# ScalarE's last copy of a chunk's first unit, placed behind the first copy of the next inner product

## The chip, the cores and the metric

The kernel runs on one core of a Trainium2 chip. The metric is the device time of one execution in microseconds (us), the median of several runs. Lower is better.

## The reference

Two blocks follow one another. The first is a retention layer: for 4 batches and 8 heads, over 768 positions of 64 dimensions, a state per head decays by a factor and takes up the outer product of key and value; the query reads it. The second is a dense pair of layers on the 3072 resulting rows of 512, with a leaky rectifier between.

```python
for t in range(S):
    state = gamma[None, :, None, None] * state + np.einsum('bhd,bhe->bhde', k[:, :, t], v[:, :, t])
    y[:, :, t] = scale * np.einsum('bhd,bhde->bhe', q[:, :, t], state)
...
h = x @ w_in                       # 512 -> 2048
g = np.maximum(0.01 * h, h)
return (g @ w_out).astype(np.float32)   # 2048 -> 512
```

## The kernel before

The sequence is cut into 6 chunks of 128 positions; with 4 batches a chunk has 512 rows. The hidden layer's 2048 columns are cut into 4 units of 512. For each chunk and unit the kernel makes the hidden values g (first layer and rectifier) and then their part of the output (second layer), which is summed over the units into a tile o of four quarters in SBUF.

All products are made by seven smaller products in place of eight, named M1 to M7, whose sums and differences are made by ScalarE and VectorE or by accumulation in PSUM. From chunk 2 on (the steady part, 4 chunks of 4 units, n = 0 to 15, chunk c = 2 + n // 4, unit u = n % 4) the first layer uses two levels of this:

- `inner_steps(n, group)` makes, one product per step, the seven inner products of one group (4 outer products in group 0, 3 in group 1). It uses PSUM banks 0 to 3. After M1, ScalarE copies bank 0 into bank 3 (line 1185, the "M1 copy"), and M6 is then accumulated into bank 3. After M5, M4, M6 and M2, ScalarE copies a bank into the SBUF tile `made` (lines 1187, 1189, 1191, 1193). M3 accumulates into the bank of M5, M7 into bank 3.
- `outer(n, group)` puts the results together on VectorE; for group 1 ScalarE applies the leaky rectifier to each quarter of g (line 1223, four activations, the "leakies").
- `output(...)` makes the second layer's seven products with `seven` (matmuls at line 662) in banks 4 to 7, in the order M1, M5, M6, M2, M7, M3, M4 (`FUSED`). M4 is the last. Its result is in bank 6, into which ScalarE has first copied M7 (line 773).
- `begin(i, ps)` takes a product into the quarter o[i]. In the first unit of a chunk (`first`, u == 0) ScalarE copies it (line 746, the "o copy"); in the later units VectorE adds it.
- `joint_visit` and `scores_of_pair` make the attention of the next chunk, in units 0 and 1 of chunks 2 to 4 ("visits"), with matmuls at lines 369, 380, 427 and 444. POOL makes a small memset in them that orders two groups of matmuls.

There is no planner. Each engine works off its own queue in the order in which the program issues instructions, and waits in that order. The main loop sets it: for unit n, the differences of g on VectorE, the inner products of group 0 for unit n + 1, a visit where there is one, then the output of unit n with the inner products of group 1 for unit n + 1 in its midst, and the last products of the output at the end of the pass. So the end of one pass and the start of the next read on ScalarE: leakies of unit n + 1, the take of M4 of unit n, the copies of the inner products of group 0 for unit n + 2.

```python
INNER = (("M1", 0, 0, 0), ("M5", 1, 3, 2), ("M4", 2, 2, 4), ("M6", 3, 4, 3), ("M2", 0, 1, 1),
         ("M3", 1, 5, 5), ("M7", 3, 6, 6))        # product, bank, weights, moving part
...
            if m == "M1":
                nc.scalar.copy(out=ps[3], in_=ps[0])
            elif m == "M5":
                nc.scalar.copy(out=sums[:, 3], in_=ps[1])
```

The weights of the inner products are streamed from DRAM into `wa` (group 0) and `wb` (group 1) by SP's queue, issued after the products that used the tile last.

Of the kernel before, what the change touches and what calls it, by code (L numbers as in the profile page):

```python
# [22 lines left out]
def kernel(  # L23
# [182 lines left out]
    def new_o(c, name="o"):  # L206
        return work.tile([128, 4, 2, N], FP32, tag=f"o{int(c > 0)}", name=f"{name}_{c}")
# [120 lines left out]
    room = {}  # L328
# [276 lines left out]
    def plus(out, a, b):  # L605
        nc.vector.tensor_tensor(out=out, in0=a, in1=b, op=ALU.add)  # L606
# [27 lines left out]
    ORDER = (0, 2, 1, 3, 4, 6, 5)  # L634
    FIRST = (0, 4, 2, 1, 3, 6, 5)
    FUSED = (0, 2, 1, 4, 5, 6, 3)
    LAST = (0, 2, 1, 3, 4, 5, 6)
# [3 lines left out]
    def seven(tiles, name, takes, takes_piece=None, order=ORDER, room=None):  # L641

        banks = {}

        def bank_of(bank):
            if bank not in banks:
                banks[bank] = room[bank] if room is not None else ffs.tile(
                    [128, 2, N], FP32, tag="ff", bufs=4, name=f"{bank}_{name}")
            return banks[bank]

        which = [("M1", "A", 0, 0), ("M6", "B", 5, 5), ("M5", "C", 4, 4), ("M4", "D", 3, 6),
                 ("M2", "A", 2, 2), ("M7", "B", 1, 1), ("M3", "C", 6, 3)]
        for m, bank, sa, sb in (which[i] for i in order):
            first = bank not in banks
            split = takes_piece is not None and bank == "C"
            ps = bank_of(bank)
            places = zip(ps, PIECES) if split else ((ps[:, i, :], (i, 0, N)) for i in range(2))
            for to, (i, a, z) in places:
                for n, (w, x, t) in enumerate(tiles):
                    rhs = x[:, sb] if sb < 4 else t[:, sb - 4]  # L660
                    for k in range(2):
                        nc.tensor.matmul(  # L662
                            to, lhsT=block(w, sa)[:, k, ts(i, 128)], rhs=rhs[:, k, a:z],
                            start=(first and (i == 0 or split) and n == 0 and k == 0),
                            stop=(n == len(tiles) - 1 and k == 1), skip_group_check=True)
                if split and m == "M3":
                    takes_piece(to, i, a, z)
            if not (split and m == "M3"):
                takes(m, ps, bank_of)
            yield  # L670
# [61 lines left out]

        return seven([(2 * u, x, t)], f"h{at}", takes, order=order)

    def output(c, o, parts, first, final, room=None, order=ORDER):

        at = f"{c}_{parts[0][0]}"
        fused = order == FUSED

        def store(i):  # L740
            if final:
                nc.sync.dma_start(out=out[c, i], in_=o[:, i])

        def begin(i, ps):
            if first:
                nc.scalar.copy(out=o[:, i], in_=ps)
            else:
                add(i, ps)

        def add(i, ps):  # L750
            plus(o[:, i], o[:, i], ps)

        def takes(m, ps, bank_of):
            if m == "M1":
                nc.scalar.copy(out=bank_of("B"), in_=ps)  # L755
            elif m == "M6":
                begin(1, ps)
            elif m == "M5":
                if isinstance(ps, list):
                    for part, (i, a, z) in zip(ps, PIECES):  # L760
                        plus(o[:, 3, i, a:z], o[:, 3, i, a:z], part)
                else:
                    begin(3, ps)
            elif m == "M4":
                begin(2, ps)
                if fused:
                    store(2)
            elif m == "M2":
                begin(0, ps)
                store(0)  # L770
            elif m == "M7":
                if fused:
                    nc.scalar.copy(out=bank_of("D"), in_=ps)  # L773
                add(3, ps)
                store(3)
                if not fused:
                    add(2, ps)
                    store(2)
            elif m == "M3":
                add(1, ps)  # L780
                store(1)

        def takes_piece(ps, i, a, z):
            plus(o[:, 1, i, a:z], o[:, 1, i, a:z], ps)
            queue = nc.scalar if 0 < a else nc.sync
            queue.dma_start(out=out[c, 1][:, i, a:z], in_=o[:, 1, i, a:z])

        return seven([(2 * u + 1, g, gd) for u, g, gd in parts], f"o{at}", takes,
                     takes_piece if final and c == NC - 1 else None, order, room)

# [9 lines left out]
    def new_g(c, u):  # L800
        i = slot[0]
        slot[0] = 1 - i
        g = work.tile([128, 4, 2, N], FP32, tag=f"g{i}", name=f"g_{c}_{u}")
        gd = work.tile([128, 3, 2, N], FP32, tag=f"gd{i}", name=f"gd_{c}_{u}")
        return u, g, gd
# [61 lines left out]
    parts = [new_g(0, 0)]  # L867
# [180 lines left out]
    def at_of(n):  # L1048
        return 2 + n // NU, n % NU
# [76 lines left out]
    for u in range(NU):  # L1126
        for c in range(2) if u > 0 else ():
            if c == 0:
                parts = []
# [38 lines left out]
    def inner(n, group, held=False):  # L1168

        products(inner_steps(n, group, held), 8)  # L1170

    def inner_steps(n, group, held=False):

        c, u = at_of(n)
        w, count = streamed[group], 4 - group
        moving = operands(c, group)
        sums = made_of[group]
        ps = [part[:, 0 : count * C].rearrange("p (i n) -> p i n", n=C) for part in bank[0:4]]
        for m, q, j, s in INNER:
            for i in range(count):  # L1180
                nc.tensor.matmul(ps[q][:, i], lhsT=w[:, j, i], rhs=part_of(moving[i], s),  # L1181
                                 start=(i == 0 and m in ("M1", "M5", "M4")), stop=True,
                                 skip_group_check=True)
# [4 lines that stand above are left out]
            elif m == "M4":  # L1188
                nc.scalar.copy(out=sums[:, 2], in_=ps[2])
            elif m == "M6":  # L1190
                nc.scalar.copy(out=sums[:, 1], in_=ps[3])
            elif m == "M2":
                nc.scalar.copy(out=sums[:, 0], in_=ps[0])
            elif m == "M3":
                plus(sums[:, 1], sums[:, 1], ps[1])
            elif m == "M7":
                plus(sums[:, 3], sums[:, 3], ps[3])
                plus(sums[:, 2], sums[:, 2], ps[3])
            yield
        if not held:  # L1200
            load_unit(n + 1, group)
# [37 lines left out]
    def products(steps, n):  # L1239

        for _ in range(n):
            next(steps, None)
# [7 lines left out]
    room = dict(zip("ABCD", map(halves, (5, 4, 7, 6))))  # L1250
# [20 lines left out]
    begun = inner_steps(1, 0, held=True)  # L1271
    for steps, leakies in ((1, later[:2]), (2, later[2:])):
        products(begun, steps)
        for do in leakies:
            do()

    for n in range(N2):
        c, u = at_of(n)
        more = n + 1 < N2
        if u == 0:  # L1280
            os[c] = new_o(c)
        visiting = c + 1 < NC and u < 2
        if n + 1 < N2:
            differences(*gs[n][1:])
        if n + 1 < N2 and u == NU - 1:
            sums_of_x(c + 1, 1)
        if n + 1 < N2:
            if n == 0:
                products(begun, 5)
            else:  # L1290
                inner(n + 1, 0, held=visiting)
            outer(n + 1, 0)
        if visiting and u == 0:
            xs[c + 1] = new_x(c + 1)
        if visiting:
            joint_visit(c + 1, 2 * u)
        steps = output(c, os[c], [gs.pop(n)], u == 0, u == NU - 1, room=room if more else last_room,
                       order=FUSED if more else LAST)
        products(steps, 3)
        if c + 1 < NC and u < 2 and following(c + 1, 2 * u):  # L1300
            scores_of_pair(*following(c + 1, 2 * u))
        if visiting:
            load_unit(n + 2, 0)
        products(steps, 1)
        if c + 1 < NC and u == 1:
            differences(*xs[c + 1])
        if c + 1 < NC and u == 2:
            sums_of_x(c + 1, 0)
        if more:
            inner(n + 1, 1)  # L1310
            for i in range(2) if visiting else ():
                ahead(c + 2, 2 * u + i)
            products(steps, 1)
            outer(n + 1, 1)
        if n + 2 == N2:
            differences(*gs[n + 1][1:])
        products(steps, 3)
# [92 lines left out]
```

## Time and profile before

| What | Value |
|---|---|
| Runs shown, median (lowest to highest) | 638.59 us (638.56 to 640.17), 4 runs |
| Profiled execution, own time | 638.57 us |
| Span of the profile | 636.8 us |
| Time around the span | 1.77 us |
| TensorE busy, and its weight loads | 630.3 us (99%), 569.2 us (89%) |
| VectorE busy | 462.5 us (73%) |
| ScalarE busy | 269.2 us (42%) |
| Granted TensorE clock, mean | 1.000 |
| M1 copies (line 1185) | 32, of 463 to 592 ns |
| o copies (line 746, by the steady part's names) | 16, of 567 to 588 ns |

The span runs from the first to the last instruction of one profiled execution. Engines are named PE (TensorE's matmuls), PEld (its weight loads, which overlap the matmuls), DVE (VectorE), ACT (ScalarE), POOL (GpSimd) and SP (SyncE). "L1185" is line 1185 of the kernel. A row of a timeline gives the start and the length in us, the engine, the line, the operation, what it writes and reads, how many instructions are merged into the row, and in brackets the idle time before it with what ended it. The ends of matmuls are modelled, so a TensorE that is busy in the page may still have been held up.

### The profile page before, as it was taken

The page shows a single profiled execution, that of the slowest core. Times are in us where ns is not written, and L with a number is a line of the kernel's source. Part 1 is how long each engine was busy: PE and PEld are TensorE (multiplying, and loading weights), DVE is VectorE, ACT ScalarE, POOL GpSimd, SP SyncE. Part 2 cuts the span into 40 slices and gives each one's busy share as a digit, 9 for nine tenths or more (in the row PEclk, how much of TensorE's full clock was granted, in tenths as well). Part 3 has the DMA queues.
Part 4 walks back from the last instruction along what each step waited for, and adds up shares of the span by engine and source line. Part 5 has one row for each costly group of instructions (what it writes and reads, how often), then busy time and mean ns, then how long its engine had stood idle before and what let it go on. Part 6 is the DMA issues. An engine that isn't in the chain of part 4 may idle for free.

```text
span 636.8 us, 14289 instructions
## 1 busy us (share of the span) xinstructions
PE 630.3 (99%) x6086; PEld 569.2 (89%) x6086; DVE 462.5 (73%) x760; ACT 269.2 (42%) x515; POOL 23.4 (4%) x45
## 2 busy tenths in 40 slices
PE   8999999999999999999999999999999999999997
PEld 5888888888888899899999999999999999999996
DVE  5689769889979977476786666877837768636655
ACT  5876556357343124242352352434333423534421
POOL 2000000000011010101000101000010000000000
PEclk9999999999999999999999999999999999999999
DMA  8931327445864998366725382864455336454301
GB/s 332 405 129 43 123 67 235 137 182 183 291 242 127 352 320 275 110 229 200 252 87 194 110 295 84 264 198 135 137 176 176 89 124 194 153 166 154 87 0 67
DMA packets 87536, 113.42 MB, mean 178 GB/s; under 512 B 3240, under 2 KB 71720, under 8 KB 87472
## 3 DMA queue, kind: packets, MB, share of 16 engines
q1 hardware_dynamic: 87168, 111.88, 53.2%
q8 instruction: 48, 0.79, 0.5%
q10 hardware_dynamic: 304, 0.62, 0.3%
q14 instruction: 16, 0.13, 0.1%
HBM read 93.35 MB, written 19.14 MB: 177 GB/s over the span
## 4 chain that ended last, share of the span: by engine, by line
PE 94%; DVE 2%; ACT 1%; DMA 1%; issue 0%; SPq 0%; DVEq 0%; ACTq 0%
PE bank L662 32%; PE bank L1181 27%; PE C_h L662 4%; PE B_o L662 4%; PE A_h L662 4%; PE C_o L662 4%; PE A_o L662 4%; PE B_h L662 4%; PE D_h L662 2%; PE D_o L662 2%; PE d L683 2%; DMA raw<-in_weights_dram 1%; PE bank L369 1%; PE bank L444 1%; PE bank L427 1%; PE bank L380 1%
## 5 line engine op out<-in xcount | busy, mean ns | idle before, releaser
L606 DVE TENSOR_TENSOR made<-made,bank 128x512 f32<-128x512 f32 (+1 forms) x96 | 56.4, 618 | 57.0 <-PE bank L1181 52.6
L606 DVE TENSOR_TENSOR o<-o,bank 128x512 f32<-128x512 f32 (+2 forms) x91 | 58.6, 661 | 53.4 <-PE bank L662 32.8
L662 PE MATMUL bank<-g,w 128*128 128x256 f32 x384 | 89.9, 382 | 0.0
L662 PEld LDWEIGHTS bank<-g,w 128*128 128x128 f32 x384 | 70.7, 190 | 9.2
L1181 PEld LDWEIGHTS bank<-x,wb 128*128 128x128 f32 x672 | 77.6, 192 | 0.8
L1181 PE MATMUL bank<-x,wb 128*128 128x128 f32 x672 | 77.6, 275 | 0.0
L1181 PE MATMUL bank<-x,wa 128*128 128x128 f32 x512 | 68.7, 276 | 0.1
L662 PE MATMUL bank<-gd,w 128*128 128x256 f32 x288 | 66.1, 379 | 0.0
L1181 PEld LDWEIGHTS bank<-x,wa 128*128 128x128 f32 x512 | 63.8, 192 | 1.9 <-ACT bank L1185 0.8
L662 PEld LDWEIGHTS bank<-gd,w 128*128 128x128 f32 x288 | 54.7, 190 | 7.4
L1181 PE MATMUL bank<-t,wa 128*128 128x128 f32 x384 | 53.3, 275 | 0.0
L1223 ACT ACTIVATE g<-g 128x512 f32<-128x512 f32 x64 | 39.3, 631 | 30.8 <-DVE g L606 30.8
L1181 PEld LDWEIGHTS bank<-t,wa 128*128 128x128 f32 x384 | 48.0, 192 | 0.0
L1185 ACT COPY bank<-bank 128x512 f32<-128x512 f32 (+1 forms) x32 | 16.7, 522 | 67.8 <-PE bank L1181 67.5
L606 DVE TENSOR_TENSOR g<-made 128x512 f32<-128x512 f32 x64 | 42.7, 688 | 1.2
L755 ACT COPY bank<-bank 128x512 f32<-128x512 f32 x17 | 9.7, 570 | 71.1 <-PE bank L662 71.0
L609 DVE TENSOR_TENSOR gd<-g,gd 128x512 f32<-128x512 f32 x48 | 33.2, 692 | 5.4 <-ACT g L1223 0.5
L773 ACT COPY bank<-bank 128x512 f32<-128x512 f32 x16 | 9.1, 570 | 46.4 <-PE bank L662 46.4
L662 PE MATMUL bank<-g,last 128*128 128x256 f32 x120 | 28.3, 380 | 0.0
L662 PE MATMUL bank<-gd,last 128*128 128x256 f32 (+1 forms) x124 | 27.5, 373 | 0.0
L662 PE MATMUL A_h<-x,w 128*128 128x256 f32 x112 | 26.6, 380 | 0.0
L662 PEld LDWEIGHTS bank<-gd,last 128*128 128x128 f32 x124 | 22.8, 190 | 3.2 <-DVE gd L609 0.3
(223 smaller groups left out, 1029.1 us busy)
## 6 DMA issues: line engine op xcount, KB each, us to landing
wa<-kept SPq DMA_DIRECT2D x16, 1344.0 KB, 7.2
raw<-in_weights_dram SPq DMA_DIRECT2D x31, 512.0 KB, 4.4
wb<-kept SPq DMA_DIRECT2D x16, 896.0 KB, 5.5
wa<-kept SPq DMA_DIRECT2D x16, 448.0 KB, 4.3
wb<-kept SPq DMA_DIRECT2D x16, 448.0 KB, 6.2
out_dram<-o SPq DMA_DIRECT2D x23, 256.0 KB, 2.5
kept<-w SPq DMA_DIRECT2D x12, 448.0 KB, 5.6
qk<-in_qk_dram SPq DMA_DIRECT2D x10, 512.0 KB, 8.6
```

Of the source, the lines that this page charges most:

```text
L369: nc.tensor.matmul(at[j][ts(h, 64), n, m, i], lhsT=x[ts(j, 64), 1, a, ts(h, 64)], rhs=x[ts(j, 64), 0, a, ts(h, 64)], start=(n == 0 and a = ...
L380: nc.tensor.matmul(sums[h][ts(j, 64), n, a], lhsT=key[ts(h, 64), 2 * a + j], rhs=val[ts(h, 64), 2 * a + j], start=(n == 0 and a == 0), sto ...
L427: mm = nc.tensor.matmul(at[n][j][ts(i, 64), m, ts(h, 64)], lhsT=by_half[h][ts(j, 64), n, a], rhs=x[ts(j, 64), 0, a, ts(h, 64)], start=(n = ...
L606: nc.vector.tensor_tensor(out=out, in0=a, in1=b, op=ALU.add)
L609: nc.vector.tensor_tensor(out=out, in0=a, in1=b, op=ALU.subtract)
L662: nc.tensor.matmul(to, lhsT=block(w, sa)[:, k, ts(i, 128)], rhs=rhs[:, k, a:z], start=(first and (i == 0 or split) and n == 0 and k == 0), ...
L683: nc.tensor.matmul(banks[r][:, i, :], lhsT=block(2 * u, r + 2 * kh)[:, k, ts(i, 128)], rhs=x[:, 2 * kh + th, k, :], start=(step == 0 and i ...
L755: nc.scalar.copy(out=bank_of("B"), in_=ps)
L773: nc.scalar.copy(out=bank_of("D"), in_=ps)
L1181: nc.tensor.matmul(ps[q][:, i], lhsT=w[:, j, i], rhs=part_of(moving[i], s), start=(i == 0 and m in ("M1", "M5", "M4")), stop=True, skip_gr ...
L1185: nc.scalar.copy(out=ps[3], in_=ps[0])
L1223: nc.scalar.activation(g[:, i], g[:, i], AF.Prelu, alpha=0.01)
```

## The change

In units with u == 0 the copy of M4 into o[2] is no longer issued when M4 is made. It is kept in a list. In the next pass the first inner product M1 and its copy are issued first; then the kept copy; then the other inner products with their copies. Only these four copies (n = 0, 4, 8, 12) change their place in ScalarE's queue. In units with u > 0, where VectorE takes M4, the list is empty and the order of instructions stays. For n = 0 the inner products of the next unit were partly issued ahead of the loop already (`begun`), and asking for 7 steps where 5 are left issues the same ones.

```diff
-    def output(c, o, parts, first, final, room=None, order=ORDER):
+    def output(c, o, parts, first, final, room=None, order=ORDER, held=None):
...
             elif m == "M4":
-                begin(2, ps)
+                if held is not None and first:
+                    held.append(lambda: begin(2, ps))
+                else:
+                    begin(2, ps)
                 if fused:
                     store(2)
...
+    held = []
     for n in range(N2):
...
         if n + 1 < N2:
-            if n == 0:
-                products(begun, 5)
-            else:
-                inner(n + 1, 0, held=visiting)
+            if n > 0:
+                begun = inner_steps(n + 1, 0, held=visiting)
+                products(begun, 1)
+            while held:
+                held.pop()()
+            products(begun, 7)
             outer(n + 1, 0)
...
         steps = output(c, os[c], [gs.pop(n)], u == 0, u == NU - 1, room=room if more else last_room,
-                       order=FUSED if more else LAST)
+                       order=FUSED if more else LAST, held=held if more else None)
```

## The prediction

> **What bounds the kernel now.** I read the page first, then the waits of the weight loads, then the order of time on the weight loads and ScalarE around the places that the waits name, and last the same stretch in a unit without that wait.
>
> From the page: the busy row of the engines, the granted clock, and the two rows of the chain that ended last.
>
> ```profile
> PE 630.3 (99%) x6086; PEld 569.2 (89%) x6086; DVE 462.5 (73%) x760; ACT 269.2 (42%) x515; POOL 23.4 (4%) x45
> PEclk9999999999999999999999999999999999999999
> PE 94%; DVE 2%; ACT 1%; DMA 1%; issue 0%; SPq 0%; DVEq 0%; ACTq 0%
> PE bank L662 32%; PE bank L1181 27%; PE C_h L662 4%; PE B_o L662 4%; PE A_h L662 4%; PE C_o L662 4%; PE A_o L662 4%; PE B_h L662 4%; PE D_h L662 2%; PE D_o L662 2%; PE d L683 2%; DMA raw<-in_weights_dram 1%; PE bank L369 1%; PE bank L444 1%; PE bank L427 1%; PE bank L380 1%
> ```
>
> TensorE is the bound, at full clock, and 94% of the chain is TensorE itself. ScalarE is busy 42%, so a copy on it costs nothing by its length. It costs only where TensorE stands still for it. The view of the waits of the weight loads has one row for the copies behind the inner product's M1 (columns: total us, times, longest):
>
> ```profile
> PEld bank L1181 <- ACT bank L1185: 0.8, 4, 0.2
> ```
>
> Four times in 32 copies. The order of time shows all four: 279.78, 381.06, 482.50 and 577.11 us. Each is the inner product that follows the first unit (u = 0) of chunks 2 to 5, and each has the copy of line 746 just ahead of the copy of line 1185. The first of them (columns: start, length, engine, line, what, count, idle before it):
>
> ```profile
> 277.53 1.23 ACT L1223 ACTIVATE g<-g 128x512 f32<-128x512 f32 x2 [0.70 <-DVE g L606]
> 277.71 1.87 PEld L1181 LDWEIGHTS bank<-x,wa 128*128 128x128 f32 x16
> 278.67 0.57 ACT L746 COPY o<-bank 128x512 f32<-128x512 f32 x1
> 279.14 0.59 ACT L1185 COPY bank<-bank 128x512 f32<-128x512 f32 x1
> 279.65 0.59 ACT L1187 COPY made<-bank 128x512 f32<-128x512 f32 x1
> 279.78 1.19 PEld L1181 LDWEIGHTS bank<-x,wa 128*128 128x128 f32 x10 [0.20 <-ACT bank L1185]
> 280.13 0.59 ACT L1189 COPY made<-bank 128x512 f32<-128x512 f32 x1
> 280.89 0.75 PEld L1181 LDWEIGHTS bank<-t,wa 128*128 128x128 f32 x6
> 281.03 0.59 ACT L1191 COPY made<-bank 128x512 f32<-128x512 f32 x1 [0.31 <-PE bank L1181]
> 281.56 0.30 PEld L1181 LDWEIGHTS bank<-x,wa 128*128 128x128 f32 x2
> ```
>
> The 16 loads are M5 and M4; the 10 after the gap are M6 (8) and the start of M2. M6 accumulates into the bank that the M1 copy fills, so it waits until that copy ends at 279.14 + 0.59 = 279.73. The M1 copy stood in ScalarE's queue behind two leaky activations and the o copy; its own input was long there (M5's loads begin at 277.71, after M1's). The same stretch one unit later, where the last second-layer product is added by VectorE and ScalarE has no o copy:
>
> ```profile
> 305.28 1.23 ACT L1223 ACTIVATE g<-g 128x512 f32<-128x512 f32 x2 [0.70 <-DVE g L606]
> 305.46 2.98 PEld L1181 LDWEIGHTS bank<-x,wa 128*128 128x128 f32 x26
> 306.42 0.58 ACT L1185 COPY bank<-bank 128x512 f32<-128x512 f32 x1
> 308.36 0.75 PEld L1181 LDWEIGHTS bank<-t,wa 128*128 128x128 f32 x6
> ```
>
> There the 26 loads run without a gap. Leakies and loads lie to each other as before (305.28 against 305.46; 277.53 against 277.71), so this unit is a model of what the change leaves: the M1 copy follows the leaky at once.
>
> **The change part by part.** Nothing is added or removed. Four ScalarE copies (n = 0, 4, 8, 12) trade places with the M1 copy of the next inner product. No DMA, no VectorE instruction and no matmul moves; SP's and POOL's queues are passed by nothing.
>
> *The M1 copy comes earlier.* From the u > 0 rows it starts 306.42 - 305.28 = 1.14 us after the pair of leakies: 277.53 + 1.14 = 278.67, which is the o copy's present start. It ends by 279.25, and with the 0.05 us from 279.73 to 279.78 M6 is free at 279.30. M6's loads are due at 277.71 + 16 x 0.1115 = 279.49 (0.1115 from 2.90 us for 26 loads). So the wait goes, with 0.19 us to spare.
>
> *What the wait is worth.* Here is the rule that I weigh. The windows from M1's first load to M7's second group of loads, with and without the wait (columns: window, length, busy us of PE, PEld, DVE, ACT, POOL, clock, DMA share, GB/s):
>
> ```profile
> 276.72:282.68 5.96, 5.95 (x52) 5.74 (x51) 4.53 (x8) 4.48 (x9) 0.00 (x0) 1.00 0.73 257
> 304.46:310.15 5.69, 5.69 (x52) 5.66 (x51) 5.14 (x9) 4.11 (x8) 0.00 (x0) 1.00 0.75 252
> ```
>
> By TensorE's busy time the window is full (5.95 of 5.96), and the change would be worth 0.01 us. The Trainium skill, "Perfetto Trace Analysis", section "Identifying the Most-Contended Engine", says that matmul occupancy misleads and that the share of weight loads should be used. By that, idle time falls from 0.22 to 0.03: 0.19 us, four times 0.76. But loads overlap (a load lasts 0.19 and they start 0.1115 apart), so this is short too. The start-to-start length decides: 5.96 - 5.69 = 0.27. From the run of loads after M1 to the second group of M2 it is 280.89 - 277.71 = 3.18 against 2.90: 0.28. The other three give 5.96, 5.96 and 5.96 again. I take 0.275 a piece, 4 x 0.275 = **1.10 us**; ends 0.8 and 1.15.
>
> A second rule would make it more. The skill's "TensorE: Matmul & The Clock Gate", section "A second HAM failure mode: psum-queue depth-cycling", tells of a kernel whose short stops between groups of matmuls let the clock swing between half and full. Part 1 of that page gives a window of about 3.4 us; one such window at half rate after each stop would be worth an estimated 4 x 1.7 = 6.8 us more. In this trace the granted clock is 1.00 in both windows, and the 10 loads after the stop keep the pace. I take nothing for it.
>
> *The o copy comes later.* It moves from 278.67 to about 279.15, behind the M1 copy. A slot is 0.47 us (278.67 to 279.14), not the 0.57 of its row. Its source bank is next written by ScalarE itself, in the copy of line 773 of the next unit (301.42); its target is next touched by VectorE's add in that unit's M4 (306 us). That is over 20 us of cover: nothing. Without cover, 0.5 us each.
>
> *The copies behind it.* Two slots remain two slots, so the M5 copy starts at 279.65 as before, and ends at 280.24. M3 writes its bank, with loads at 281.56 - 0.28 = 281.28: about 1.0 us to spare. The M4 copy also stays; it gives ScalarE free for the M6 copy at about 280.6, and M6 is ready at 281.03 - 0.28 = 280.75. Nothing is pushed.
>
> *A wait passed on.* The o copy now stands behind the M1 copy's wait for M1. M1 is done before the leakies end (278.76), so it waits for nothing; if it did, only this copy and the M5 copy would be behind. All later waits, and the SP issues that TensorE releases, shift with TensorE. After the inner product VectorE waits 1.34 us for M3, then 1.06.
>
> Sum: the profiled execution took 638.57 us (span 636.8, 1.77 around it). 638.57 - 1.10 = 637.47; its time is 0.02 under the median shown, so **637.5** holds for either. That is 0.17%, just under the 0.2% that a measurement of this kernel can tell from no change.
>
> **The rivals.**
>
> *More than the wait* (over 1.28 us). Three visits follow a boundary. In the second, POOL's small memset came 0.94 us after the one before it, against 0.60 and 0.61 in the other two; the 32 loads of line 444 took 0.73 us there against 0.56. Nothing in ScalarE or VectorE explains it. If the shift of 0.28 us undoes it, 0.17 more is won: 637.3. The same chance runs the other way, in two places. A further tenth from the pace after a stop, which the rows model, would also do it. Chance 0.26, at 637.2.
>
> *A part only.* M6 has 0.19 us to spare. If the M1 copy's start slips by 0.3 us, 0.1 us of wait stays at each, 638.0; if the copy is not moved past in effect (a dependence ties both to the same release), 638.6. The u > 0 units, where the copy does start at once in this same company, speak against it. Chance 0.08.
>
> *Slower.* The M5 copy is third behind the leakies, as now, but TensorE arrives 0.28 us earlier at M3, which overwrites its bank. Wait there decides once the M5 copy is over 1.0 us later than now. For a loss of 1.28 us net each boundary needs 0.32 + 0.28 = 0.60 us of wait, so the copy 1.6 us later: 639.9. That is more than three extra slots of ScalarE, and the change adds none. Chance 0.04, and 0.01 for weights that land late: in the second such unit the larger load took 8.6 us from its issue at 395.48, so to 404.1, and is used at 406.23; it is issued behind TensorE's progress and shifts with it.
>
> **How the numbers follow.** The forecast, all four waits gone and nothing in their place: 0.61, at 637.3 to 637.75 (ends 0.8 to 1.25 us). More: 0.26. A part or nothing: 0.08. Slower: 0.05. The range 637.1 to 638.1 leaves out the slower case, half of the partial one and the far end of the first. Faster by over 0.2% is under 637.3: 0.26; slower by over 0.2%: 0.05; between them 0.69.
>
> **What would show it.** In the profile after, the row of weight loads waiting for the copy behind M1 is gone. At the four places the copy of line 1185's counterpart starts about 1.14 us after the pair of leakies, the o copy 0.47 us behind it, and the M5 copy as late as now; 26 loads stand in one run of 2.98 us. The four windows are 5.69 long, and the span is near 635.7. A row of M3 waiting for the M5 copy would prove the slower rival; visit loads of 0.56 or 0.73 us in other places, the first. If the waits are gone and the span is not shorter by 1 us, my step from wait to span is wrong.

## The result and the profile after

| | before | after |
|---|---|---|
| Median | 638.82 us (59 runs) | 637.91 us (39 runs) |
| Lowest | 638.48 us | 637.46 us |
| Ratio of the times, with its 95% interval | | 0.9985 (0.998 to 0.9989) |
| Span of the profiled execution | 636.8 us | 635.9 us |

The change makes the kernel faster by 0.15%, or some 0.96 us; the interval reaches from 0.7 to 1.3 us. The forecast was 1.10 us, 637.5 us, and the measured 637.91 lies in its range. The 59 runs of the kernel before that are counted here have a median 0.23 us above that of the four shown first.

Line numbers past 765 moved: the inner matmuls are now at line 1184, the M1 copy at 1188, the copies of M5, M4, M6 and M2 at 1190 to 1196, the leakies at 1226. The page after, engines and clock:

```profile
PE 629.0 (99%) x6086; PEld 568.8 (89%) x6086; DVE 463.7 (73%) x760; ACT 269.1 (42%) x515; POOL 23.3 (4%) x45
PEclk9999999999999999999999999999999999999999
```

Little is to be seen there: TensorE's busy time is 1.3 us less, at the same clock. What happened is in the view of the waits of the weight loads. All its rows that name a PSUM bank of the steady part (columns: total us, times, longest):

```profile
PEld bank L369 <- issue: 2.0, 6, 0.3
...
PEld bank L662 <- DVE gd L609: 0.3, 1, 0.3
...
PEld bank L427 <- DVE made L606: 0.3, 1, 0.3
...
PEld bank L1184 <- ACT made L1194: 0.2, 1, 0.2
```

The row for the M1 copy, 0.8 us in four waits, is gone, and no row of the steady part is new; the four above were there before. A boundary is, from here on, one of the four places where the inner product behind a chunk's first unit begins. The timeline of the first, weight loads and then ScalarE:

```profile
277.91 2.98 PEld L1184 LDWEIGHTS bank<-x,wa 128*128 128x128 f32 x26
280.81 0.75 PEld L1184 LDWEIGHTS bank<-t,wa 128*128 128x128 f32 x6
281.49 0.30 PEld L1184 LDWEIGHTS bank<-x,wa 128*128 128x128 f32 x2
...
277.73 1.23 ACT L1226 ACTIVATE g<-g 128x512 f32<-128x512 f32 x2 [0.70 <-DVE g L606]
278.87 0.58 ACT L1188 COPY bank<-bank 128x512 f32<-128x512 f32 x1
279.39 0.58 ACT L746 COPY o<-bank 128x512 f32<-128x512 f32 x1
279.87 0.58 ACT L1190 COPY made<-bank 128x512 f32<-128x512 f32 x1
280.34 0.60 ACT L1192 COPY made<-bank 128x512 f32<-128x512 f32 x1
281.24 0.59 ACT L1194 COPY made<-bank 128x512 f32<-128x512 f32 x1 [0.30 <-ACT made L1192]
```

The 26 loads of M5, M4, M6 and the start of M2 stand in one run. The M1 copy follows the pair of leakies by 1.14 us, the o copy it by 0.52, and the M5 copy starts 2.14 us after the leakies (279.87 - 277.73), against 2.12 before. The window of the first boundary, 5.96 us long before, and that of the unit without an o copy, 5.69 long before (columns as before):

```profile
276.92:282.61 5.69, 5.69 (x52) 5.66 (x51) 4.53 (x8) 4.46 (x9) 0.00 (x0) 1.00 0.75 254
304.39:310.08 5.69, 5.69 (x52) 5.67 (x51) 5.13 (x9) 4.11 (x8) 0.00 (x0) 1.00 0.73 246
```

The windows of the other three boundaries, 5.96 us before, are 5.69 each as well. For a sum over all four I take a stretch that leaves out the varying start of the program: from the first loads of line 369 in the first pass of the loop to the loads that wait for VectorE in the last unit. In the kernel before, and then in the one after:

```profile
263.20 1.02 PEld L369 LDWEIGHTS bank<-o 64*64 64x64 f32 x64 [0.33 <-issue]
622.42 5.08 PEld L662 LDWEIGHTS bank<-gd,last 128*128 128x128 f32 x28 [0.34 <-DVE gd L609]
```

```profile
263.40 1.02 PEld L369 LDWEIGHTS bank<-o 64*64 64x64 f32 x64 [0.33 <-issue]
621.54 5.08 PEld L662 LDWEIGHTS bank<-gd,last 128*128 128x128 f32 x28 [0.34 <-DVE gd L609]
```

622.42 - 263.20 = 359.22 us, and 621.54 - 263.40 = 358.14: 1.08 us less, which is four times 0.27. This "loop stretch" is the measure for the experiments too, since the part ahead of it moved from 263.1 to 264.6 us over the profiles of this study, a spread larger than the effect. Three profiles of the changed kernel agree in it to 0.02 us; of the kernel before there is one profile.

### The profile page after: what moved, and what is told of

It is laid out like the page before. It is cut to its first block, busy times and chain, and to the rows that moved or that the text cites. A ratio compares the mean times of both kernels' runs of the same rounds, so it can differ in the third digit from the quotient of the medians.

```text
span 635.9 us, 14285 instructions
## 1 busy us (share of the span) xinstructions
PE 629.0 (99%) x6086; PEld 568.8 (89%) x6086; DVE 463.7 (73%) x760; ACT 269.1 (42%) x515; POOL 23.3 (4%) x45
## 4 chain that ended last, share of the span: by engine, by line
PE 95%; DVE 2%; ACT 1%; DMA 1%; issue 0%; DVEq 0%; ACTq 0%
PE bank L662 32%; PE bank L1184 27%; PE C_h L662 4%; PE B_o L662 4%; PE A_h L662 4%; PE C_o L662 4%; PE A_o L662 4%; PE B_h L662 4%; PE D_h L662 2%; PE D_o L662 2%; PE d L683 2%; PE bank L369 1%; PE bank L444 1%; PE bank L427 1%; PE bank L380 1%; DMA t<-decay_dram 1%
```

## The experiments

The theory: the gain is the wait of M6 for the M1 copy at four places and nothing else, and it passes to the time one for one. The rivals: part of it is given back; the o copy's or the M5 copy's new place matters by itself; the place of the work on ScalarE or VectorE matters.

| Kernel | Loop stretch | Against before | Median | Ratio (95%) |
|---|---|---|---|---|
| before | 359.22 | | 638.82 to 639.09 | 1 |
| after | 358.14 | -1.08 | 637.91 | 0.9985 (0.998 to 0.9989) |
| e1_again | 358.12 | -1.10 | 637.96 | 0.998 (0.9966 to 0.9993) |
| e2_vector | 358.21 | -1.01 | 638.23 | 0.999 (0.9975 to 1.0005) |
| e3_last | 358.21 | -1.01 | 637.77 | 0.9979 (0.997 to 0.9989) |
| e4_twice | 361.69 | +2.47 | 641.50 | 1.0035 (1.0025 to 1.0046) |
| e5_half | 358.66 | -0.56 | 638.50 | 0.9991 (0.998 to 1.0002) |
| e6_two | 358.14 | -1.08 | 637.97 | 0.9981 (0.9972 to 0.999) |
| e7_three | 359.47 | +0.25 | 639.33 | 1.0006 (0.9997 to 1.0014) |
| e8_four | 361.94 | +2.72 | 641.52 | 1.0038 (1.0026 to 1.0051) |
| e9_leaky | 358.13 | -1.09 | 637.22 | 0.9969 (0.9958 to 0.998) |
| e10_again | 358.14 | -1.08 | 638.17 | 0.9985 (0.9973 to 0.9997) |

Times in us. The edits of e2 and e4 are to the kernel before, those of the others to the changed kernel; e1 and e10 are the changed kernel itself. The place that e9 changes lies ahead of the loop stretch. The intervals of e2, e5 and e7 hold 1; for these the loop stretch decides.

**e1_again: the changed kernel, beside e2 to e4.** 

> The changed kernel once more, beside the others. Theory (the whole gain is M6's wait for the M1 copy, 0.27 us at each of four places): 1.1 us under before, a ratio of 0.9983. Rival (part of the gain is lost or given back elsewhere): 0.5 to 0.8 us under before.

The stretch is 1.10 us shorter, the median 1.06 (639.02 to 637.96). The rival of a part given back is not seen in the stretch.

**e2_vector: VectorE takes the copy at its old place.**

```diff
             elif m == "M4":
-                begin(2, ps)
+                if first and fused and c >= JOINED:
+                    nc.vector.tensor_copy(out=o[:, 2], in_=ps)
+                else:
+                    begin(2, ps)
```

> In the kernel before, VectorE instead of ScalarE copies M4 into o[2] in the first unit of chunks 2 to 5, at the old place; ScalarE's queue is free of it. Theory: the same 1.1 us under before, since only the M1 copy's start counts; M6's wait is gone and VectorE's differences of g move 0.6 us later into its 1.34 us of idle time. Rival (the gain needs the copy to stay on ScalarE, because VectorE then becomes late for the visit): under half of the gain, with a new wait of line 427 or 662 for VectorE.

The stretch is 1.01 us shorter and no wait takes the place of the one removed, though the run's ratio alone would not tell it from no change. Its timeline, ScalarE and then VectorE:

```profile
278.05 1.23 ACT L1226 ACTIVATE g<-g 128x512 f32<-128x512 f32 x2 [0.70 <-DVE g L606]
279.19 0.58 ACT L1188 COPY bank<-bank 128x512 f32<-128x512 f32 x1
...
279.13 0.68 DVE L766 COPY o<-bank 128x512 f32<-128x512 f32 x1
...
283.16 2.11 DVE L606 TENSOR_TENSOR made<-made,bank 128x512 f32<-128x512 f32 x3 [0.56 <-PE bank L1184]
```

The M1 copy comes 1.14 us after the leakies, as in the change. VectorE's idle time ahead of M3's add is 0.56 us, where it was 1.34 before and 1.06 in the change: the copy is paid from there. So the gain does not hang on ScalarE keeping the copy, nor on where the copy goes.

**e3_last: the kept copy behind all the inner copies.**

```diff
-            while held:
-                held.pop()()
             products(begun, 7)
+            while held:
+                held.pop()()
```

> The kept copy goes behind all five copies of the inner product instead of behind the first only. Theory: the same as the change, 1.1 us under before, as nobody waits for the o copy. Rival (the copies behind the kept one matter, so M5's copy coming 0.47 us earlier wins something more): 1.3 us under before or better.

1.01 us in the stretch, so the M5 copy's start 0.48 us earlier wins nothing. The 0.07 us by which e2 and e3 fall short of the change arise ahead of the moved copy: in both, M1's first two groups of loads start 0.42 us apart in place of 0.32 at the first boundary, and the windows of the other three are 5.68 to 5.69 us as in the change. What makes that one slip was not tried.

**e4_twice: the copy twice at its old place.**

```diff
                 begin(2, ps)
+                if first and fused and c >= JOINED:
+                    begin(2, ps)
```

> In the kernel before, the o copy is made twice at its old place, so that the M1 copy comes one slot of 0.47 us later still. Theory: M6's wait grows from 0.27 to 0.74 us at each of four places, 4 x 0.47 = 1.9 us over before, a ratio of 1.0030. Rival (the wait is partly hidden or made good later by TensorE): under 1.0 us over before.

It came out 2.47 us over before in the stretch and 2.48 in the medians, more than the 1.9 expected. The timeline says why:

```profile
280.09 1.19 ACT L746 COPY o<-bank 128x512 f32<-128x512 f32 x2
281.17 0.59 ACT L1187 COPY bank<-bank 128x512 f32<-128x512 f32 x1
...
281.82 1.19 PEld L1183 LDWEIGHTS bank<-x,wa 128*128 128x128 f32 x10 [0.81 <-ACT bank L1187]
```

The M1 copy starts 1.08 us after the first o copy, against 0.47 with one: a repeat of the same copy takes 0.61 us and not a slot of 0.47. With 0.61 the wait row says the same: 0.81 - 0.20 = 0.61. Four times 0.61 is 2.44 us. So the wait passes to the time one for one, as the theory has it, and the size that I gave the second copy was wrong.

**e5_half: kept back at two of the four places.**

```diff
-                       order=FUSED if more else LAST, held=held if more else None)
+                       order=FUSED if more else LAST, held=held if n in (0, 8) else None)
```

> The changed kernel with the copy kept back after chunks 2 and 4 only (n = 0 and 8); after chunks 3 and 5 it stays at its old place. Theory: two of the four waits remain, so 0.55 us under before and as much over the change. Rival (the gain comes from one of the places or from the program as a whole): the full 1.0 us or none.

0.56 us in the stretch. Two waits of 0.20 us are left, at 381.62 and 577.39 us, the two places where the copy was not kept back. The gain is additive by place.

**e6_two, e7_three, e8_four: the kept copy made two, three and four times.** These measure the spare time behind the M1 copy, on which the rival "slower" of the prediction rests.

```diff
             while held:
-                held.pop()()
+                do = held.pop()
+                for _ in range(2):       # 3 and 4 in the others
+                    do()
```

> The changed kernel with the kept copy made twice behind the M1 copy. A repeat onto the same target costs 0.61 us. Theory: M5's copy ends 0.61 us later (281.06 in the timeline of the change), still 0.4 us ahead of M3's loads at 281.49: no wait, the same time as the change, about 1.0 us under before. Rival (the copies behind the M1 copy are as critical as it is): 4 x 0.61 = 2.4 us over the change.

> The kept copy made three times, so M5's copy ends 1.22 us later, at 281.67. Theory: M3 waits 0.23 us and M7 0.08 more for the M6 copy, four times 0.3: about 1.2 us over the change, level with before. Rival (spare time for M3 is more than I worked out): the same as the change; (none at all): 4.9 us over it.

> The kept copy made four times, so M5's copy ends 1.83 us later. Theory: M3 waits 0.84 us at each place and M7 some 0.08 more, four times 0.92: 3.7 us over the change, 2.6 over before, with a row of M3's loads waiting for ScalarE. Rival (VectorE or the visit behind it gives some of it back): under 2.5 us over the change.

Over the change the stretch grew by 0.00, 1.33 and 3.80 us, where 0, 1.2 and 3.7 were expected. The first loads of M1, the M5 copy and the loads of M3 that wait for it, in the kernel with three copies and then in the one with four:

```profile
277.17 0.41 PEld L1184 LDWEIGHTS bank<-x,wa 128*128 128x128 f32 x2
...
281.36 0.59 ACT L1190 COPY made<-bank 128x512 f32<-128x512 f32 x1
...
282.00 0.30 PEld L1184 LDWEIGHTS bank<-x,wa 128*128 128x128 f32 x2 [0.18 <-ACT made L1190]
```

```profile
276.62 0.41 PEld L1184 LDWEIGHTS bank<-x,wa 128*128 128x128 f32 x2
...
281.42 0.59 ACT L1190 COPY made<-bank 128x512 f32<-128x512 f32 x1
...
282.06 0.30 PEld L1184 LDWEIGHTS bank<-x,wa 128*128 128x128 f32 x2 [0.80 <-ACT made L1190]
```

With two copies M3 does not wait, with three and four it does. Counted from M1's first loads, the M5 copy starts 2.95 us behind in the change (279.87 - 276.92), 4.19 with three copies and 4.80 with four; M3's loads start 4.57, 4.83 and 5.44 us behind. So the M5 copy is 1.24 and 1.85 us late, and M3 is 0.26 and 0.87: in both kernels 0.98 us of lateness is free, and all beyond it is lost. From the third copy to the fourth each place costs (3.80 - 1.33) / 4 = 0.62 us, the whole repeat. The edge lies where I had put it, at about 1 us, and the change stands well ahead of it.

**e9_leaky and e10_again: the same idea at one more place.** The profile after still has a wait of M7 for the M6 copy (0.2 us) and of a visit for VectorE (0.3 us), both just ahead of the loop. There ScalarE idles ahead of the M1 copy and has two leakies between the copies of M4 and M6.

```diff
-    for steps, leakies in ((1, later[:2]), (2, later[2:])):
+    later[0]()
+    for steps, leakies in ((1, later[1:3]), (2, later[3:])):
```

> The changed kernel, and the same idea at the one place that the loop does not cover: ahead of the loop, the first leaky of the unit goes ahead of the M1 copy of the begun inner product (ScalarE waits 3.48 us there), and the third goes ahead of M5's copy, so that only the fourth stands between M4's and M6's copies. In the profile of the change M7 waits 0.23 us there for the M6 copy, and the visit behind it 0.32 us for VectorE, which waited 0.53 us for a leaky. Theory: queue order on ScalarE is all that these waits are; both go, 0.5 us under the change, 1.5 under before. Rival (VectorE or the tile that M5's copy overwrites sets both waits): the same as the change.

> The changed kernel once more, on the same chip as the one beside it. Both theories: 0.9 to 1.1 us under before.

The times are counted from M1's first load to the first loads of line 369 in the loop: 263.58 - 249.34 = 14.24 us in e9, and 263.86 - 249.19 = 14.67 in e10 and 263.40 - 248.73 = 14.67 in the profile after. That is 0.43 us less, where 0.5 was expected. The loads of M7 and of the visit, in the profile after and then in e9:

```profile
254.50 0.30 PEld L1184 LDWEIGHTS bank<-x,wa 128*128 128x128 f32 x2 [0.23 <-ACT made L1194]
...
256.23 0.56 PEld L427 LDWEIGHTS bank<-qk,states 64*64 64x64 f32 x32 [0.32 <-DVE made L606]
```

```profile
254.80 0.30 PEld L1184 LDWEIGHTS bank<-x,wa 128*128 128x128 f32 x2
...
256.41 0.56 PEld L427 LDWEIGHTS bank<-qk,states 64*64 64x64 f32 x32 [0.19 <-DVE made L606]
```

M7's wait is gone. The visit's wait is not, against what was expected: it fell from 0.32 to 0.19 us. Counted from M1's first load, M7's loads come 0.31 us earlier than in the profile after (254.80 - 249.34 = 5.46, in place of 254.50 - 248.73 = 5.77), and the sums of VectorE for which the visit waits begin 0.43 us earlier (255.68 - 249.34 = 6.34, in place of 255.50 - 248.73 = 6.77), so the visit still waits for VectorE and gains what VectorE gained. The median was 637.22 us against 638.17 for the change beside it, ratio to before 0.9969 (0.9958 to 0.998) against 0.9985 (0.9973 to 0.9997). These two intervals overlap, but that alone does not make the kernels equal: five of the six runs of e9 lie below the lowest of the twelve beside it, 637.55 us. That e9 is the faster is likely, then; how much it wins, 0.95 us by the medians or 0.43 by the profile, stays open, and the 0.43 are what I would count on.

## Why the prediction was right

*The wait.* M6's wait for the M1 copy is gone at all four places. M6 had 0.19 us to spare by my sum, and the loads indeed run through. The three other signs came within some hundredths: the M1 copy 1.14 us behind the leakies as forecast, the o copy 0.52 behind it in place of 0.47, and the M5 copy 2.14 behind the leakies in place of 2.12.

*What it was worth.* I had the choice between 0.01 us a place by matmul occupancy, 0.19 by the idle time of the weight loads and 0.275 start to start. The stretch gave 1.08 / 4 = 0.27. The rule of the Trainium skill ("Perfetto Trace Analysis", section "Identifying the Most-Contended Engine") led away from the misleading row, but the sum by weight loads, 0.76 us, would have been 0.32 us too small. The window's TensorE occupancy was full before (5.95 of 5.96) and after (5.69 of 5.69), although the longer window held 0.27 us of waiting.

*From wait to span.* The prediction asked for a span shorter by 1 us, near 635.7, or else its step from wait to span would be wrong. The span came out 635.9, shorter by 0.9. The step holds all the same: the part ahead of the loop took 0.20 us more in this profile (263.40 against 263.20), and the loop stretch, which has the waits, took 1.08 less.

*Clock.* The windows show 1.00 before and after, and nothing beyond the wait was won. In e4 and e8, where the stops are 0.8 us long, the clock in the window is 1.00 too. So taking nothing for the rule on clock swings was right for stops of this length.

*The o copy's new place* costs nothing: e3 moves it further and e2 takes it off the engine, and both stay within 0.1 us of the change in the stretch.

*The copies behind it.* About 1.0 us to spare for M3 was the step that spoke against the rival "slower". e7 and e8 measure it as 0.98 us.

*The rival of more than the wait* fell. The second visit's late memset was not undone by the shift. In the profile after:

```profile
386.15 0.10 POOL L408 MEMSET between<- 128x1 f32 x1 [0.96 <-PE bank L444]
```

It was 0.94 before. In all twelve profiles it is 0.94 to 0.96 us in this visit and 0.60 or 0.61 in the two others. So it comes with the place in the program and not by chance of timing; what makes it late was not tried.

*The time itself.* 637.91 against 637.5: 0.23 us of this is the median of before, 638.82 in 59 runs where the four shown had 638.59. The rest, 0.18 us, is the difference of the medians, 0.91, against the forecast gain. The stretch gives 1.08, and the two repeats of the changed kernel 1.06 and 0.92 by medians. The interval of the ratio, 0.7 to 1.3 us, holds all of these; which is nearest the truth for unprofiled runs stays open.

## What to carry to other kernels

On an engine that works in order, look not for how busy it is but for which of its instructions another engine is waiting for, and put the ones nobody waits for behind it; here 42% busy ScalarE still held up TensorE four times. Cost such a wait start to start against the same stretch without it, as occupancy hides it and idle gaps of overlapping loads understate it. Then count the spare time of what comes next: here the next copy could be late by about 1 us, and two copies more there took back the whole gain.

## What was not expected of the hardware

A ScalarE copy of 128x512 out of PSUM that repeats the copy just ahead, with the same source and the same target, starts 0.61 us after it in e4, when the row of the first, 0.57 to 0.59 us long, has ended. In e8 four such copies take 2.43 us. A copy with another source and another target starts 0.47 to 0.48 us after one into SBUF, 0.1 us before the row ahead of it ends. Whether the same source or the same target makes the difference, and whether it is the engine or an ordering wait in the program, was not tried.
